# Both heads' sums from the exponentials, x rounded on VectorE, and attention visits by twos in an attention and gated feed-forward kernel

## The chip, the cores and the metric

The kernel runs on one core of a Trainium2 chip. The core has a matrix engine (TensorE, PE in the profile), three engines for elementwise work (VectorE or DVE, ScalarE or ACT, GpSimd or POOL), and SyncE (SP), which here issues the DMA transfers in order. Each engine runs its own instructions in order and waits for other engines by semaphores. Operands lie in SBUF, results of matmuls in PSUM, and large arrays in DRAM. The metric is the device time of one execution in microseconds.

## The reference

Causal attention over a sliding window of 64 positions feeds a gated feed-forward layer:

```python
# q, k, v: 8 batches, 8 heads, 576 positions, 64 values; float32
scores = matmul(q, k.T) / sqrt(64)
scores = where((rel >= 0) & (rel < 64), scores, -1e9)      # rel: position of q minus position of k
attn = exp(scores - max(scores))
attn = attn / (sum(attn) + 1e-9)
x = matmul(attn, v)                                        # laid out as 4608 tokens x 512
gate = 1 / (1 + exp(-(x @ w_gate)))                        # 512 x 1536
out = (gate * (x @ w_val)) @ w_out                         # 1536 x 512
```

The three weight arrays come as 64-bit floats; all else is float32, and so is the result.

## The kernel before

**Tiles and numbers.** The 4608 tokens stand in 12 tiles of 384, taken in 6 pairs of tiles s = 0 to 5. The 8 heads stand in 4 pairs p. A tile with a pair of heads is a unit of attention, written (t, p): eight units for a pair of tiles. Matmuls that need float32 accuracy split both operands into a rounded part and a remainder and make three products of them; a rounded part is a conversion to the type fp32r, a remainder is one subtraction behind it.

**A unit of attention** goes over the engines so. TensorE makes the scores of both heads (L224) in blocks of 128x128. VectorE scales and masks a block and takes its minimum (L249, with a read of the minimum). ScalarE takes the exponential (L257) and, where `accum_out` is given, the row's sum with it, which a second short instruction reads out (ACTIVATION_READ_ACCUMULATOR). VectorE inverts the sums (L264, L265), GpSimd or VectorE multiplies (L274), TensorE transposes (L328), ScalarE copies the transposes to SBUF (L333), TensorE multiplies them with v (L358). In the first two tiles the second head's exponentials leave no sum; VectorE adds it up with a reduction instead (L270). There the outputs of L358 become a tile of x directly: ScalarE rounds them out of PSUM (L365), VectorE subtracts (L366).

**The order of the whole.** The first pair's attention comes first, on its own. Then come its up products (L394), gate and product (L402, L407), the split of the hidden values (L420, L422) and its down products (L442); the weights are meanwhile converted from their 64-bit halves, in a step a on ScalarE (L117, L118), a step b on VectorE (L126, L128, L130) and a step c (ScalarE's rounding L158, VectorE's remainder L159, and stores). From the second pair on, up and down products are made by a scheme of seven products for eight (`product`, L619; k = 0 to 5 numbers blocks of the hidden size, n = 0 to 6 the products), with sums of weights that GpSimd makes in the second pair (L541 to L547, split by L554 and L561) out of rows loaded again from DRAM (L531), and weights loaded for each k and n (L468). The attention of the next pair of tiles is fed in between these products. Such a place is called a visit here; a dictionary `fill` holds them under the key ("u", 7k + n), and `attend` puts them into the order.

Two forms of visit exist. `stage_s` takes one unit: the outputs of the unit before it, then its own scores, copies and exponentials, its normalization and transposes later. `stage_v` takes two units at once, and copies a whole 128x384 tile of outputs (L311) where `stage_s` copies three pieces (L289, L290, L295). The second pair of tiles uses `stage_s`, later pairs `stage_v`.

What sets the order: every step is put into a table of events with a time, a rank and a function; the table is sorted, and the language's scheduler then places instructions by its own simulated times. Matmuls keep the order of the program. `tc.issue_after(ins)` places instructions behind `ins` on the engine of `ins` only; the conversions of weights use it with `marks`, where each tile of x leaves the instructions that made it.

## Time and profile before

| | |
|---|---|
| median of three runs | 949.63 us (948.51 to 950.33) |
| the profiled execution | 950.16 us, of which 948.2 are the span from first to last instruction |
| granted TensorE clock, mean | 0.997 |
| busy: PE, PEld, DVE | 934.0, 898.5, 712.2 us |
| busy: ACT, POOL | 502.7, 150.7 us |
| DMA | 273.45 MB, mean 288 GB/s |

A row of a timeline gives the start, the length, the engine, the line of the kernel, the operation, result and operands, the shape and the number of instructions taken together; in square brackets stand the idle time before it and what ended it. Rows of groups give busy time and mean nanoseconds of one instruction. The length of an instruction overlaps the next one's start by some hundredths to a tenth of a microsecond, so that a pitch is read from start to start. SPq stands for SP's issues of transfers, and a DMA's landing is counted from its issue.

### The profile page before, as it was taken

To read this page: it belongs to the slowest core of one execution; us is meant where nothing else is said; L and a number is where in the kernel's file an instruction comes from. 1 tells how busy PE (TensorE), PEld (TensorE's weight loads), DVE (VectorE), ACT (ScalarE), POOL (GpSimd) and SP (SyncE) were. 2 spreads that over 40 slices of the span, in tenths; PEclk is the share of its full clock that TensorE was granted. 3 is DMA by queue.
4 is the path that set the end of the run, shared out by engine and by line. 5 is a ranking of instruction groups with operands and counts; after the bars stand their busy time and mean duration, and the time that the engine had idled before them with its cause. 6 is when DMAs were issued, how large, how long until landed. Compare 5 with 4: busy or idle time off the path is not lost.

```text
span 948.2 us, 20297 instructions
## 1 busy us (share of the span) xinstructions
PE 934.0 (99%) x7164; PEld 898.5 (95%) x7164; DVE 712.2 (75%) x1919; ACT 502.7 (53%) x1374; POOL 150.7 (16%) x232
## 2 busy tenths in 40 slices
PE   6999999999999999999999999999999999999998
PEld 5899999889999999999999999999999999999998
DVE  6989989787888975666875677786566796566882
ACT  7866776655666653545553455454455565222460
POOL 4201104604773000311000113000111100000000
PEclk9999999999999999999999999999999999999999
DMA  9899998989999988888879788788888678988474
GB/s 327 311 383 358 368 321 282 359 292 358 386 315 315 407 288 288 287 271 270 264 252 317 251 291 290 258 251 296 287 267 269 221 247 273 299 260 250 130 214 164
DMA packets 105509, 273.45 MB, mean 288 GB/s; under 512 B 11456, under 2 KB 33600, under 8 KB 105408
## 3 DMA queue, kind: packets, MB, share of 16 engines
q1 hardware_dynamic: 105408, 272.15, 85.4%
q8 instruction: 57, 0.93, 0.4%
q14 instruction: 44, 0.36, 0.1%
HBM read 220.20 MB, written 51.90 MB: 287 GB/s over the span
## 4 chain that ended last, share of the span: by engine, by line
PE 92%; DMA 4%; DVE 3%; ACT 1%; issue 0%; SPq 0%; DVEq 0%; ACTq 0%
PE pr L619 45%; PE y L619 23%; PE ph L394 10%; PE y L442 4%; PE pp L328 3%; PE pr L358 2%; PE s L224 1%; DMA raw<-in_moe_w_gate_dram 1%; PE pr L224 1%; DMA a<-w32d 1%; DMA wt<-wd 1%; PE oo L358 1%; DMA wd<-ws 1%; PE s L358 1%; DVE p L249 1%; DMA out_dram<-yo 0%
## 5 line engine op out<-in xcount | busy, mean ns | idle before, releaser
L619 PE MATMUL pr<-x_T,wt 128*128 128x384 f32 x1224 | 224.4, 335 | 0.0
L619 PE MATMUL y<-h,wot 128*128 128x384 f32 x1260 | 220.4, 335 | 0.0
L619 PEld LDWEIGHTS y<-h,wot 128*128 128x128 f32 x1260 | 218.3, 188 | 1.3 <-DVE h L407 1.2
L619 PEld LDWEIGHTS pr<-x_T,wt 128*128 128x128 f32 x1224 | 212.6, 188 | 0.3 <-issue 0.3
L619 PE MATMUL pr<-x_B,wt 128*128 128x384 f32 x1008 | 188.7, 338 | 0.6 <-DMA wt<-wd 0.6
L619 PEld LDWEIGHTS pr<-x_B,wt 128*128 128x128 f32 x1008 | 174.4, 188 | 3.3 <-issue 2.1
L701 ACT CAST h<-h 128x384 fp32r<-128x384 f32 x210 | 104.8, 514 | 97.7 <-PE y L619 42.7
L274 POOL TENSOR_TENSOR p<-p,rs 128x384 f32<-128x384 f32 x76 | 69.4, 926 | 524.6 <-DVE rs L265 388.5
L702 DVE TENSOR_TENSOR h<-h,h 128x384 fp32r<-128x384 f32 x210 | 110.2, 552 | 23.4 <-ACT h L701 23.1
L257 ACT ACTIVATE p<-p,mn 128x128 f32<-128x128 f32 x288 | 110.8, 392 | 19.8 <-DVE mn L249 19.1
L394 PE MATMUL ph<-x,w 128*128 128x384 f32 x576 | 106.1, 338 | 0.1
L402 ACT ACTIVATE g<-c 128x384 f32<-128x384 f32 x90 | 46.9, 522 | 108.0 <-DVE c L658 96.2
L394 PEld LDWEIGHTS ph<-x,w 128*128 128x128 f32 x576 | 99.8, 188 | 2.6 <-issue 1.0
L629 DVE TENSOR_TENSOR c<-pr,p 128x384 f32<-128x384 f32 x60 | 33.0, 551 | 46.4 <-PE pr L619 46.4
L407 DVE SCALAR_TENSOR_TENSOR h<-g,c 128x384 f32<-128x384 f32 x90 | 50.1, 557 | 5.9 <-DVE c L658 0.5
L333 ACT COPY p<-pp 128x384 f32<-128x384 f32 x80 | 34.4, 479 | 30.6 <-PE pp L328 29.8
L257 ACT ACTIVATION_READ_ACCUMULATOR p<-p,mn 128x1 f32 x264 | 49.8, 189 | 0.0
L634 ACT COPY p<-pr 128x384 f32<-128x384 f32 x60 | 27.2, 472 | 37.8 <-PE pr L619 37.8
L629 DVE TENSOR_TENSOR u<-pr,p 128x384 f32<-128x384 f32 x60 | 33.1, 552 | 16.0 <-PE pr L619 15.8
L328 PE MATMUL pp<-ident,p 128*128 128x128 f32 x288 | 41.6, 281 | 1.8 <-POOL p L274 1.3
L658 DVE TENSOR_TENSOR c<-pr,p 128x384 f32<-128x384 f32 x60 | 33.1, 555 | 10.2 <-PE pr L619 9.8
L619 PE MATMUL pr<-x_T,ws 128*128 128x384 f32 x216 | 40.3, 338 | 0.0
(186 smaller groups left out, 1216.9 us busy)
## 6 DMA issues: line engine op xcount, KB each, us to landing
wt<-wd SPq DMA_DIRECT2D x186, 512.0 KB, 4.5
wot<-wod SPq DMA_DIRECT2D x105, 512.0 KB, 4.6
v<-in_vN_dram SPq DMA_DIRECT2D x48, 384.0 KB, 5.6
wd<-ws SPq DMA_DIRECT2D x48, 256.0 KB, 5.1
k<-in_kT_dram SPq DMA_DIRECT2D x48, 224.0 KB, 5.9
q<-in_qT_dram SPq DMA_DIRECT2D x48, 192.0 KB, 5.7
w32d<-w SPq DMA_DIRECT2D x36, 256.0 KB, 5.0
wd<-w SPq DMA_DIRECT2D x36, 256.0 KB, 5.6
```

What stands on the lines that cost most here:

```text
L257: exp = nc.scalar.activation(pt[:, u, :], pt[:, u, :], AF.Exp, bias=mn[:, u:u + 1], scale=-1.0, **sums)
L274: eng.tensor_mul(out=pt, in0=pt, in1=rs.unsqueeze(2).broadcast_to([P, UP, P]))
L328: pe(nc.tensor.transpose(pp[:, u, :], pt[:, u, :], ident))
L358: pe(nc.tensor.matmul(oo[U // 2][h * BLK:(h + 1) * BLK, U % 2 * BLK:(U % 2 + 1) * BLK], vt[:, U, h * BLK:(h + 1) * BLK], pT[h][:, U // 2, ...
L394: pe(nc.tensor.matmul(ph, l, r, start=i == 0, stop=i == len(prs) - 1))
L402: act = nc.scalar.activation(g, c, AF.Tanh)
L407: nc.vector.scalar_tensor_tensor(out=out, in0=g, scalar=1.0, in1=val, op0=ALU.add, op1=ALU.mult)
L442: pe(nc.tensor.matmul(yb[y], l, r, start=first and n == 0, stop=last and n == 2))
L619: pe(nc.tensor.matmul(ps, l, r, start=first and i == 0, stop=last and i == 2, skip_group_check=not check))
L629: marks["plus"] = nc.vector.tensor_add(out=o, in0=ps, in1=a).ins
L701: nc.scalar.copy(h2[:, 0, :], src)
L702: nc.vector.tensor_sub(out=h2[:, 1, :], in0=src, in1=h2[:, 0, :].bitcast(F32))
```

## The change

Four edits stand in it.

1. In the first two tiles both heads' exponentials give their sums; the eight reductions L270 are gone, and 24 more sums are read out on ScalarE.
2. x is rounded by VectorE, which also subtracts: the conversion out of PSUM leaves ScalarE.
3. What a tile of x leaves in `marks` is now the last copy of transposes on ScalarE and both of VectorE's instructions. A weight conversion that was to stand behind a tile of x thereby stands behind the copy on ScalarE, and behind the split on VectorE.
4. In the second pair of tiles the visits at 4 and 9 stay single; from 19 on they are `stage_v`: units 3 and 4 are taken at 19 (with the outputs of unit 2), units 5 and 6 at 26, unit 7 at 33, and the last outputs at 40. Before, single visits stood at 14, 19, 25, 30 and 35, and the last outputs at 41. `stage_v` now also takes one unit or none.

```diff
-                sums = {} if t < 2 and h else {"accum_out": rs[:, u:u + 1]}
                 exp = nc.scalar.activation(pt[:, u, :], pt[:, u, :], AF.Exp, bias=mn[:, u:u + 1],
-                                           scale=-1.0, **sums)
+                                           scale=-1.0, accum_out=rs[:, u:u + 1])
...
     def normalize(t, p, h):
         pt, rs = st[(t, p, h)], sums_of[(t, p)][:, h, :]
-        if t < 2 and h:
-            nc.vector.reduce_sum(out=rs, in_=pt, axis=mybir.AxisListType.X)
         if t < 4:
             invert(rs)
...
-            c, d = new
+            c, d = new[0], new[-1]
...
-            scores(*d, (True, False, True) * 2)
+            if len(new) > 1:
+                scores(*d, (True, False, True) * 2)
             scores(*c)
...
-            for u in (d, c):
+            for u in new[::-1]:
...
     def x_split(src, nm, i, eng):
         x2 = xp.tile([P, 2, TT], F32R, name=f"x_{nm}", tag=f"x{i}")
-        hi = nc.scalar.copy(x2[:, 0, :], src)
+        hi = eng.tensor_copy(out=x2[:, 0, :], in_=src)
         lo = eng.tensor_sub(out=x2[:, 1, :], in0=src, in1=x2[:, 0, :].bitcast(F32))
-        marks[nm] = (hi.ins, lo.ins)
+        marks[nm] = (marks["pTv"], hi.ins, lo.ins)
...
-    VISITS = (4, 9, 14, 19, 25, 30, 35)
...
-            for v, u in enumerate(VISITS, 1):
+            for v, u in enumerate((4, 9), 1):
                 visit(("u", u), 3, *unit(s + 1, v), unit(s + 1, v - 1), u % NPR)
                 visit(("u", u + 1), 4, *unit(s + 1, v))
                 visit(("u", u + 3.5), 1, *unit(s + 1, v))
-            visit(("u", 41), 2, *unit(s + 1, 7))
+            for u, new, done in ((19, (3, 4), (2,)), (26, (5, 6), (3, 4)), (33, (7,), (5, 6)), (40, (), (7,))):
+                new, done = ([unit(s + 1, i) for i in x] for x in (new, done))
+                visit(("u", u), 5, new, done)
+                for a, tn, tb in zip(new[::-1], (1.5, 2.5), (3.5, 5)):
+                    visit(("u", u + tn), 4, *a)
+                    visit(("u", u + tb), 1, *a)
```

Three places where instructions move. First ScalarE, at the last unit of the first pair, (1, 3), whose exponentials are `p_1_3`; `oo` are outputs of L358, `w` and `raw` belong to the weight conversion. Before:

```order
L257 ACTIVATE p_1_3_751<-p_1_3_751,mn_1_3_752 128x128 x2
L365 CAST x_0_724<-oo_0_711 128x384
L257 ACTIVATE p_1_3_751<-p_1_3_751,mn_1_3_752 128x128
L333 COPY pT_1_1_731<-pp_1_1_727 128x384
L333 COPY pT_1_1_737<-pp_1_1_733 128x384
L365 CAST x_1_795<-oo_1_782 128x384
L117 ACTIVATE w_0_1_838<-raw_1_336 128x512
L118 ACTIVATE raw_1_336<-raw_1_336 128x512
L333 COPY pT_1_2_802<-pp_1_2_798 128x384
L333 COPY pT_1_2_808<-pp_1_2_804 128x384
L333 COPY pT_1_3_814<-pp_1_3_810 128x384
L333 COPY pT_1_3_820<-pp_1_3_816 128x384
```

The same place with the change:

```order
L256 ACTIVATE p_1_3_744,rs_3_734<-p_1_3_744,mn_1_3_745 128x128 x3
L331 COPY pT_1_1_724<-pp_1_1_720 128x384
L331 COPY pT_1_1_730<-pp_1_1_726 128x384
L117 ACTIVATE w_0_1_830<-raw_1_334 128x512
L118 ACTIVATE raw_1_334<-raw_1_334 128x512
L331 COPY pT_1_2_794<-pp_1_2_790 128x384
L331 COPY pT_1_2_800<-pp_1_2_796 128x384
L331 COPY pT_1_3_806<-pp_1_3_802 128x384
L331 COPY pT_1_3_812<-pp_1_3_808 128x384
```

The casts of x have left the queue, and the weight conversion L117, L118 follows the copies of unit 1 directly.

Second VectorE behind the last exponentials of that unit; x_0 to x_3 are tile 1's four parts of x. Before:

```order
L366 TENSOR_TENSOR x_0_724<-oo_0_711,x_0_724 128x384
L270 TENSOR_REDUCE rs_3_741<-p_1_3_751 128x3
L264 SCALAR_TENSOR_TENSOR rs_3_741<-rs_3_741 128x3
L407 SCALAR_TENSOR_TENSOR h_0_0_776<-g_0_671,ph_0_0_763 128x384
L265 RECIPROCAL rs_3_741<-rs_3_741 128x3
L420 CAST hh_0_778<-h_0_0_776 128x384
L422 TENSOR_TENSOR hl_0_779<-h_0_0_776,hh_0_778 128x384
L366 TENSOR_TENSOR x_1_795<-oo_1_782,x_1_795 128x384
L126 TENSOR_SCALAR zz_1_841<-w_0_1_838 128x512
L128 SCALAR_TENSOR_TENSOR w_0_1_838<-w_0_1_838,zz_1_841 128x512
L130 ISA w_0_1_838<-raw_1_336,w_0_1_838 128x1024
L159 TENSOR_TENSOR w_1_845<-w_0_1_838,w_1_845 128x2x256
```

With the change, from the last inversion on:

```order
L405 SCALAR_TENSOR_TENSOR h_0_0_768<-g_0_665,ph_0_0_755 128x384
L418 CAST hh_0_770<-h_0_0_768 128x384
L363 CAST x_1_787<-oo_1_774 128x384
L420 TENSOR_TENSOR hl_0_771<-h_0_0_768,hh_0_770 128x384
L364 TENSOR_TENSOR x_1_787<-oo_1_774,x_1_787 128x384
L126 TENSOR_SCALAR zz_1_833<-w_0_1_830 128x512
L128 SCALAR_TENSOR_TENSOR w_0_1_830<-w_0_1_830,zz_1_833 128x512
L363 CAST x_2_827<-oo_2_814 128x384
L130 ISA w_0_1_830<-raw_1_334,w_0_1_830 128x1024
L364 TENSOR_TENSOR x_2_827<-oo_2_814,x_2_827 128x384
L363 CAST x_3_855<-oo_3_842 128x384
L364 TENSOR_TENSOR x_3_855<-oo_3_842,x_3_855 128x384
```

The conversions of x (L363) now stand between, and the remainder of the weight (L159) comes behind x_3, where it stood ahead of x_2.

Third SP's queue at k = 3 of the second pair. `wt_1_3_4` are the weights of product n = 4, `a0` and `a1` rows of weights for GpSimd's sums, `wd` stores, q, k and v inputs of units. Before:

```order
L531 DMA a1_1_4_3843<-w32d_1_10_135 128x512
L481 DMA wd_3_6_176<-ws2_1_3_3917 128x512
L180 DMA q_5_1_4183<-in_qT_dram 128x384
L468 DMA wt_1_3_4_3930<-wd_3_4_174 128x1024
L531 DMA a0_0_5_4010<-w32d_0_5_118 128x512
L468 DMA wt_1_3_5_3943<-wd_3_5_175 128x1024
L181 DMA k_5_1_4184<-in_kT_dram 128x448
```

With the change:

```order
L479 DMA wd_3_6_176<-ws2_1_3_3871 128x512
L180 DMA q_4_3_3996<-in_qT_dram 128x384
L529 DMA a1_1_4_3869<-w32d_1_10_135 128x512
L181 DMA k_4_3_3997<-in_kT_dram 128x448
L180 DMA q_5_1_4000<-in_qT_dram 128x384
L181 DMA k_5_1_4001<-in_kT_dram 128x448
L466 DMA wt_1_3_4_3884<-wd_3_4_174 128x1024
L529 DMA a0_0_5_4004<-w32d_0_5_118 128x512
L466 DMA wt_1_3_5_3901<-wd_3_5_175 128x1024
```

Loads for two units, q and k each, stand ahead of the weights of n = 4, with the row block L529 among them; before, one q did.

## The prediction

> **What bounds the kernel now.** I read the busy times on the page first, then the start by windows, then the timelines of the two places that the change touches, engine by engine.
>
> ```profile
> span 948.2 us, 20297 instructions
> PE 934.0 (99%) x7164; PEld 898.5 (95%) x7164; DVE 712.2 (75%) x1919; ACT 502.7 (53%) x1374; POOL 150.7 (16%) x232
> ```
>
> TensorE is busy for 99% of the span. Where it has idle time and who is late there, the windows of the start show (columns: stretch, its length, busy time of PE, PEld, DVE, ACT, POOL, then granted clock, DMA share, GB/s):
>
> ```profile
> 10.00:20.00 10.00, 8.92 (x128) 6.80 (x121) 8.22 (x48) 9.63 (x34) 4.94 (x6) 1.00 1.04 399
> 20.00:30.00 10.00, 8.84 (x119) 7.51 (x119) 9.93 (x54) 9.75 (x37) 3.98 (x6) 0.83 1.01 374
> 30.00:40.00 10.00, 9.11 (x133) 7.55 (x133) 8.78 (x31) 7.71 (x24) 4.09 (x5) 1.00 0.88 333
> 40.00:50.00 10.00, 10.00 (x77) 9.62 (x74) 9.10 (x18) 8.30 (x16) 0.00 (x0) 1.00 0.85 267
> ```
>
> From 10 to 30 us VectorE and ScalarE are both full; at 30 to 40 both have gaps, and TensorE is 0.89 us short. From 40 on TensorE has no idle time: there a gain needs fewer or denser matmuls, while before that it needs TensorE's inputs sooner. The stretch from 30 to 40 is the last unit of the start, tile 1 with head pair 3. How TensorE comes out of it, in an order that the change leaves alone:
>
> ```profile
> 38.79 2.05 PE L358 MATMUL oo<-pT,v 128*64 128x64 f32 x48 [0.61 <-ACT pT L333]
> 40.77 8.81 PE L394 MATMUL ph<-x,w 128*128 128x384 f32 x48
> ```
>
> The outputs of units 2 and 3 (48 matmuls) end at 40.77, and the first up products that need tile 1 begin. A faster start has to move this row.
>
> **The start: what the three edits cost.** Prices, by groups:
>
> ```profile
> L270 DVE TENSOR_REDUCE rs<-p 128x3 f32<-128x384 f32 x8 | 4.3, 540 | 1.4 <-ACT p L257 1.4
> L365 ACT CAST x<-oo 128x384 fp32r<-128x384 f32 x8 | 3.6, 466 | 1.0 <-PE oo L358 1.0
> L366 DVE TENSOR_TENSOR x<-oo,x 128x384 fp32r<-128x384 f32 x8 | 4.3, 544 | 0.6 <-ACT x L365 0.6
> L420 DVE CAST h<-h 128x384 fp32r<-128x384 f32 x10 | 3.8, 380 | 0.1
> L257 ACT ACTIVATION_READ_ACCUMULATOR p<-p,mn 128x1 f32 x264 | 49.8, 189 | 0.0
> ```
>
> VectorE loses eight reductions (L270) and gains eight conversions out of PSUM, which before does not show. The nearest rows are L420, the same conversion out of SBUF (0.380 us), and L366, the subtraction that reads the same PSUM tile (0.544 us). I take L366's price since its source is the one the new instruction reads; then eight for eight is a wash (0.54 against 0.54). At L420's price VectorE gains 8 x 0.16 = 1.3 us, of which only what falls in the last unit reaches the end. A rule of the Trainium skill bears on it, *VectorE: DVE Perf Modes*, section "Why PSUM operands drop a tier": an operand in PSUM keeps fp32 work at the basic rate. By it the price is L366's and the sum the one below; without it the price is L420's and the sum that of rival 1. The pair of rows fits the rule, but the trace of before has no such conversion.
>
> ScalarE loses eight casts and gains 24 accumulator reads. With and without a read the exponentials stand like this:
>
> ```profile
> 32.50 0.40 ACT L257 ACTIVATE p<-p,mn 128x128 f32<-128x128 f32 x1 [1.17 <-DVE mn L249]
> 33.67 0.68 ACT L257 ACTIVATE p<-p,mn 128x128 f32<-128x128 f32 x2
> 34.26 0.46 ACT L365 CAST x<-oo 128x384 fp32r<-128x384 f32 x1
> 34.62 0.40 ACT L257 ACTIVATE p<-p,mn 128x128 f32<-128x128 f32 x1
> 36.75 0.48 ACT L365 CAST x<-oo 128x384 fp32r<-128x384 f32 x1 [1.00 <-PE oo L358]
> 37.13 0.69 ACT L117 ACTIVATE w<-raw 128x512 f32<-128x512 f32 x1
> 38.28 1.60 ACT L333 COPY pT<-pp 128x384 f32<-128x384 f32 x4
> ```
>
> Three with a read take 1.17 (32.50 to 33.67, the two behind the first being left out here), 0.39 each; two without take 0.59 (33.67 to 34.26), 0.30 each. A read adds 0.09, 24 add 2.2, and the casts give back 8 x 0.36 (34.26 to 34.62) = 2.9. Before 32 us lie 21 of the reads (1.9) and some six of the casts (2.2): next to nothing on ScalarE, nothing on VectorE, so I leave the last unit's first exponential where it is, at 32.50.
>
> Behind it ScalarE does six exponentials with reads, 32.50 + 6 x 0.39 = 34.84 (before 34.92: 34.62 + 0.30, with a cast between), and two copies of unit 2's transposes (0.40 each, from the four at 38.28) until 35.6. Before, it then stood 1.00 us for the outputs of unit 2 because the cast of x came ahead of the first weight conversion. Now that cast is VectorE's, and the conversion (L117 and L118, 37.13 to 38.28, 1.15) fills the hole: done at 36.75 where it was 38.28. What the four copies behind it wait for then is the last head's normalized exponentials:
>
> ```profile
> 31.56 0.46 DVE L264 SCALAR_TENSOR_TENSOR rs<-rs 128x3 f32<-128x3 f32 x1
> 35.22 0.54 DVE L270 TENSOR_REDUCE rs<-p 128x3 f32<-128x384 f32 x1
> 36.85 1.07 DVE L422 TENSOR_TENSOR hl<-h,hh 128x384 fp32r<-128x384 f32 x1
> 41.56 1.01 DVE L366 TENSOR_TENSOR x<-oo,x 128x384 fp32r<-128x384 f32 x2
> 42.95 0.69 DVE L128 SCALAR_TENSOR_TENSOR w<-w,zz 128x512 int32<-128x512 int32 x1
> 43.55 0.42 DVE L126 TENSOR_SCALAR zz<-w 128x512 int32<-128x512 int32 x1
> 43.89 0.68 DVE L130 CUSTOM_DVE_ANT_0 w<-raw,w 128x1024 uint16<-128x1024 uint16 x1
> 36.68 0.83 POOL L274 TENSOR_TENSOR p<-p,rs 128x384 f32<-128x384 f32 x1 [1.51 <-DVE rs L265]
> ```
>
> That multiplication ends at 37.51. With the sums ready at 34.9, VectorE inverts them by about 35.7 and POOL ends at 36.6; transposes, copies from 36.95 to 38.5, outputs, and TensorE could start the up products at about 39.4, 1.4 earlier than 40.77.
>
> But those products need all four tiles of x, and VectorE is now the maker of both halves. Its queue from 35.7 on, at the pitches of the rows above (0.45 for a conversion or subtraction, from the two that take 1.01 together; L128 0.60 and L126 0.34 from start to start; L130 0.60, its length being L128's): the gate product, which reads PSUM too, 36.2; h's conversion, held beside POOL until 36.6, to 37.1; x_1 37.55; h's remainder 38.0; x_1's remainder 38.45; L126 38.8; L128 39.4; x_2 39.85; L130 40.45; x_2's remainder 40.9; x_3 41.35; its remainder 41.8. The eleventh of the first twelve up products needs this last one, so the twelve end at 41.8 + 2 x 0.17 = 42.15. Before, the last remainder landed at 41.56 + 1.01 = 42.57, and the twelve ended at about 42.9. **Gain 0.8 us.** Bounds: 1.4 if VectorE keeps up; 0 if the queue up to 32 us gets longer by what is saved here, or if the weights, converted in the order of arrival behind it, come no earlier. A loss is rival 3.
>
> **The visits by twos.** One single visit in the second pair of tiles, and one double visit as they stand in the third:
>
> ```profile
> 219.37 2.24 PE L619 MATMUL pr<-x_B,wt 128*128 128x384 f32 x12
> 225.41 2.24 PE L619 MATMUL pr<-x_B,ws 128*128 128x384 f32 x12
> 227.49 2.24 PE L619 MATMUL pr<-x_B,wt 128*128 128x384 f32 x12
> 390.31 2.25 PE L619 MATMUL pr<-x_T,wt 128*128 128x384 f32 x12
> 392.49 1.62 PE L358 MATMUL pr<-p,v 128*64 128x64 f32 x48
> 394.04 0.67 PE L224 MATMUL pr<-k,q 64*64 64x128 f32 x16
> 395.51 4.45 PE L619 MATMUL pr<-x_B,wt 128*128 128x384 f32 x24
> 399.80 3.29 PE L619 MATMUL pr<-x_T,wt 128*128 128x384 f32 x18
> ```
>
> Twelve dense products take 227.49 - 225.41 = 2.08. From 219.37 to 225.41 lie 24 of them and one single visit: 6.04 - 4.16 = 1.88. From 390.31 to 399.80 lie 36 and a double one: 9.49 - 6.24 = 3.25, which is 1.55 of outputs, 1.47 of scores and 0.23 of entering and leaving. Replaced are five single visits, 5 x 1.88 = 9.40, by three: one unit's outputs with two units' scores, half of 1.55 plus some 0.08 of its own start, 0.85 + 1.47 + 0.23 = 2.55; 3.25; and two units' outputs with one unit's scores, 1.55 + 0.80 + 0.23 = 2.58. Together 8.38; the last unit's outputs stay alone. **Gain 1.0 us.** The matmuls stay, so only entering and leaving is saved. Bounds: 1.5 if the first and the third visit enter and leave for nothing (0.23 each); 0 if products behind a double visit wait for its copies, which in the row at 395.51 they don't (24 in 4.29, twice 2.08 and 0.13).
>
> The visits' work on VectorE and ScalarE is the same in number; TensorE covers it with the products between visits. SP's queue, though, is reordered: the load of the weights for k=3, n=4 (L468) now stands behind the loads of unit 4's k and of unit 5's q and k, and behind a load (L531) that waits for POOL to give a buffer back. As it was, POOL's splitting of one set of sums, SP's issue, the product, and the landing times of L468 in this stretch:
>
> ```profile
> 255.93 2.15 POOL L561 TENSOR_TENSOR ws<-sw,ws 128x128 fp32r<-128x128 f32 x4
> 266.09 0.38 SPq L468 DMA_DIRECT2D wt<-wd  x1
> 274.13 2.24 PE L619 MATMUL pr<-x_B,wt 128*128 128x384 f32 x12
> DMA to landing us min/median/max: 5.3/6.6/10.6
> ```
>
> Issued at 266.09 and taking 6.6, it landed at about 272.7, 1.4 ahead of its product. In the change that product comes earlier by 0.8 from the start and by 1.88 for the single visit at 25 that falls away, less 2.55 - 1.88 = 0.67 for the bigger one at 19: at 274.13 - 2.0 = 272.1. If the buffers come free no later than TensorE's own earlier progress gives them, the issue is earlier by about 0.7 as well, lands at 272.0, and the product waits for nothing. I price it at nothing; the cover is 0.1 us wide, and its cost without is the slower rival.
>
> **Sum.** The profiled execution took 950.16 (span 948.2, and 2.0 around it), 0.53 above the median of the three, 949.63. -0.8 - 1.0 = -1.8: 948.4 against its own time, and **947.8** against the median.
>
> **Rivals.** (1) *The whole start gain comes through*, 1.4, because the conversion out of PSUM costs nearer to L420's 0.380, and up to 32 us VectorE gains some of the 1.3 as well: 949.63 - 1.0 - 1.4 to 2.5 = 946.1 to 947.2, take 946.8. For it: VectorE at 9.93 is the fuller engine. Against: ScalarE is as full, 9.75.
> (2) *Nothing comes of the start*, since VectorE has the same work and the conversions end when they did: 948.6. For it: the equal prices; against: the 1.00 us hole on ScalarE at 36.75 does go.
> (3) *VectorE is shut out while POOL multiplies.* The inversion at 31.56 takes 0.46 for 128x3 elements and the subtraction at 36.85 takes 1.07 against 0.54 of the group of L366, ending 0.41 behind POOL's multiplication (37.51). A reduction is not held so (35.22, 0.54). Without reductions in between, the second head's inversion falls into the first head's multiplication in each of seven units; at 0.3 to 0.5 each, a third of it on the path, that is 7 x 0.4 / 3 = 0.9, which eats the start's 0.8: 948.7; with all of it on the path, 7 x 0.4 = 2.8, and 950.6. The Trainium skill has this, *SBUF — State Buffer*, section "Who interferes with whom": VectorE with two SBUF inputs and GpSimd exclude one another for a whole instruction, and a reduction never takes part; the rows agree.
> (4) *Slower: TensorE waits for the weights of k=3, 4 and 5 behind the loads of the double visits.* The place is the queue above: SP issues in order, so a load that waits for its buffer holds the weights. POOL now splits one set of sums (the 2.15 at 255.93) before it makes the sums whose buffer the load L531 waits for. If the whole chain of these loads comes 2.15 later by that, and two issues more stand ahead of the weights (2 x 0.38), the cover of 0.1 leaves 2.8 us of waiting at k=3; at each of the next two k one q and one k more stand ahead, 0.76 less the 0.1: 0.7. Together 4.2: 949.63 - 1.8 + 4.2 = 952.0. It decides once the waits sum to more than 1.8, for k=3 alone from an issue after 272.1 - 6.6 + 1.8 = 267.3. For it: three loads more stand ahead. Against: before, the median landing left 1.4 us to spare.
>
> **How the numbers follow.** About 0.2% (1.9 us) is what a measurement of this kernel can tell from no change: faster is below 947.7, slower above 951.5. Forecast (-1.2 to -2.4) 0.42, of which 0.22 lie below 947.7; rival 1 0.22, all faster; rival 2 0.18, no change; rival 3 0.06, no change; rival 4 0.12, slower. So faster 0.44, same 0.44, slower 0.12. The range 946.0 to 950.3 leaves out rival 4 and the far ends of rivals 1 and 3; the forecast's own is 947.2 to 948.5.
>
> **What would show it.** The first twelve up products of tile 1 end 0.8 earlier than 42.9 (1.4: rival 1; not earlier: rival 2). The conversion L117 stands at 35.6 with no wait for the outputs ahead. The new conversion's mean is near 0.54. The three double visits add 2.55, 3.25 and 2.58 to the dense products around them. A wait of TensorE for weights at k=3, n=4 is rival 4; inversions of 0.4 us and more are rival 3. I am wrong if the start moves by over 1.5 either way, if the visits save under 0.5, or if TensorE has a new wait of over 0.5.

## The result and the profile after

| | before | changed |
|---|---|---|
| median | 949.63 us (948.51 to 950.33) | 954.81 us (953.60 to 957.17) |
| ratio | 1 | 1.0057 [1.0046, 1.0068] |
| the profiled execution | 950.16, span 948.2 | 953.82, span 952.0 |
| granted TensorE clock, mean | 0.997 | 1.000 |

The change is slower by 5.2 us; 947.8 was forecast, and the time lies outside the predicted range. The profiled execution is the lowest but one of its five, 1.0 below their median, and that of the kernel before lay 0.5 above its own. So the spans differ by 3.8 us only, and some 1.4 of the medians' 5.2 stand in neither trace. The page of the changed kernel:

```profile
span 952.0 us, 20303 instructions
PE 931.3 (98%) x7164; PEld 895.8 (94%) x7164; DVE 712.8 (75%) x1919; ACT 501.6 (53%) x1380; POOL 150.5 (16%) x232
```

TensorE has the same 7164 matmuls and less busy time than before (931.3 against 934.0); what is longer is its waiting. The windows of the changed kernel say where (columns as in the prediction):

```profile
50.00:60.00 10.00, 9.18 (x67) 7.69 (x65) 6.11 (x18) 5.98 (x14) 0.00 (x0) 1.00 0.90 328
70.00:80.00 10.00, 9.24 (x88) 8.23 (x87) 9.49 (x22) 6.32 (x13) 0.00 (x0) 1.00 1.03 383
80.00:90.00 10.00, 8.04 (x48) 7.55 (x47) 9.16 (x28) 8.67 (x26) 2.39 (x2) 1.00 1.02 379
```

Two of the same stretches before:

```profile
50.00:60.00 10.00, 10.00 (x75) 9.27 (x74) 8.03 (x26) 7.03 (x18) 0.00 (x0) 1.00 1.00 372
80.00:90.00 10.00, 10.00 (x71) 9.05 (x71) 9.73 (x21) 6.10 (x17) 1.93 (x2) 1.00 0.99 361
```

From 40 to 90 us TensorE had no idle time before. Now it has 0.82 between 50 and 60, 0.76 between 70 and 80 and 1.96 between 80 and 90, and in the first of these VectorE too did less than before, 6.11 against 8.03. The order of TensorE's products is the same but for the visits, so that the start of each can be set against the start of the same one before (minus is earlier):

| start before, us | 40.8 | 44 | 60 | 67 | 76 | 84 | 89 | 229 | 329 | end |
|---|---|---|---|---|---|---|---|---|---|---|
| shift, us | -1.39 | -0.85 | +1.06 | +1.09 | +2.05 | +4.25 | +4.04 | +3.97 | +3.82 | +3.80 |

The start came 0.85 earlier. Then 1.9 us went between 44 and 60, and 2.95 between 67 and 89; the visits (229 to 329) brought back 0.15. The rows of TensorE in the changed kernel that carry this:

```profile
39.39 2.34 PE L392 MATMUL ph<-x,w 128*128 128x384 f32 x10
41.88 6.85 PE L392 MATMUL ph<-x,w 128*128 128x384 f32 x38
...
53.86 2.73 PE L392 MATMUL ph<-x,w 128*128 128x384 f32 x14
56.74 2.60 PE L392 MATMUL ph<-x,w 128*128 128x384 f32 x12 [0.16 <-DVE w L159]
60.12 2.02 PE L392 MATMUL ph<-x,w 128*128 128x384 f32 x10 [0.78 <-DVE w L159]
...
74.62 0.45 PE L356 MATMUL ph<-p,v 128*64 128x64 f32 x8 [0.76 <-ACT g L400]
...
77.99 6.43 PE L392 MATMUL ph<-x,w 128*128 128x384 f32 x36
86.39 2.36 PE L392 MATMUL ph<-x,w 128*128 128x384 f32 x12 [1.96 <-ACT g L400]
```

and in the kernel before, where none of these waits stands:

```profile
54.52 6.54 PE L394 MATMUL ph<-x,w 128*128 128x384 f32 x36
...
75.95 8.55 PE L394 MATMUL ph<-x,w 128*128 128x384 f32 x48
```

Below, the loss between 44 and 60 is called the first part (up products of the third block wait for weights), that between 67 and 89 the second part (at 74.62 outputs of a visit, at 86.39 up products wait for a gate that has still to read the PSUM bank they write).

**The first part.** VectorE of the changed kernel, from 50 us on:

```profile
54.59 0.43 DVE L126 TENSOR_SCALAR zz<-w 128x512 int32<-128x512 int32 x1 [3.32 <-ACT w L117]
54.93 0.68 DVE L128 SCALAR_TENSOR_TENSOR w<-w,zz 128x512 int32<-128x512 int32 x1
...
56.00 0.68 DVE L159 TENSOR_TENSOR w<-w,w 128x512 fp32r<-128x512 f32 x1
...
59.38 0.68 DVE L159 TENSOR_TENSOR w<-w,w 128x512 fp32r<-128x512 f32 x1
```

The program's names say whose these are. The step at 54.59 belongs to `w_2_1`, weights of a down product; the one at 54.93 to `w_1_2`, 56.00 is the remainder of `w_0_2` and 59.38 that of `w_1_2`, both of which the up products need next. In the order before, `w_1_2`'s L128 (51.83) and `w_0_2`'s remainder (53.46) stand ahead of `w_2_1`, whose L126 comes at 54.34; the last row is `w_1_2`'s remainder:

```profile
51.83 0.69 DVE L128 SCALAR_TENSOR_TENSOR w<-w,zz 128x512 int32<-128x512 int32 x1
53.46 0.69 DVE L159 TENSOR_TENSOR w<-w,w 128x512 fp32r<-128x512 f32 x1 [0.95 <-ACT w L158]
...
56.35 0.68 DVE L159 TENSOR_TENSOR w<-w,w 128x512 fp32r<-128x512 f32 x1
```

`w_2_1` was late because ScalarE, in its own order, stood for a load ahead of it (the row at 53.14, raw weights of `w_1_3`):

```profile
53.14 0.68 ACT L118 ACTIVATE raw<-raw 128x512 int32<-128x512 uint32 x1 [2.60 <-DMA raw<-in_moe_w_val_dram]
53.89 0.66 ACT L117 ACTIVATE w<-raw 128x512 f32<-128x512 f32 x1
54.46 0.61 ACT L158 CAST w<-w 128x512 fp32r<-128x512 f32 x1
```

So VectorE stood 3.32 us at a step that nobody needed yet, with the steps behind it that TensorE did need. `w_1_2` was ready at 59.38 + 0.68 = 60.06 instead of 57.03, three later.

A second swap bears on the same weights, on ScalarE. The first step of `w_0_3`, which waits for a store, now stands ahead of the rounding of `w_1_2` (58.06):

```profile
57.11 0.67 ACT L117 ACTIVATE w<-raw 128x512 f32<-128x512 f32 x1 [1.35 <-DMA w32d<-w]
```

Before, the rounding came first (55.40, L117 at 56.30). In the change VectorE ended its step b of `w_1_2` only at 57.9, so that the two swaps hold the rounding about equally long; e9 and e14 below tell them apart.

**The second part.** ScalarE of the changed kernel around the gate of tile 1's block 3, and the same gate before:

```profile
80.07 0.40 ACT L256 ACTIVATE p<-p,mn 128x128 f32<-128x128 f32 x1 [2.17 <-DVE mn L249]
...
84.80 0.60 ACT L158 CAST w<-w 128x512 fp32r<-128x512 f32 x1
85.31 0.65 ACT L117 ACTIVATE w<-raw 128x512 f32<-128x512 f32 x1
85.87 0.46 ACT L400 ACTIVATE g<-ph 128x384 f32<-128x384 f32 x1
```

```profile
76.63 0.40 ACT L257 ACTIVATE p<-p,mn 128x128 f32<-128x128 f32 x1 [0.63 <-DVE mn L249]
...
81.61 0.48 ACT L402 ACTIVATE g<-ph 128x384 f32<-128x384 f32 x1
```

The gate starts 4.26 later: 3.44 because the exponentials ahead of it start later (they wait for VectorE's minima; VectorE did 1.9 us less between 50 and 60 than before, and from 66 us to those minima it worked with only 0.5 of idle time), and 0.82 because two steps of conversions, the rounding of `w_2_3` (84.80) and L117 of `w_1_5` (85.31), now stand ahead of the gate on ScalarE. TensorE itself was 2.04 late at that point (77.99 against 75.95). 4.26 - 2.04 = 2.22, less some 0.25 that it had to spare before, is the wait of 1.96. The 0.76 at 74.62 is the same thing one gate earlier: the gate of tile 0's block 3 starts 2.05 later than before (74.10 against 72.05), where TensorE was 1.09 late. ScalarE had stood 1.16 for VectorE at the rounding of `w_2_2` (70.38), which now goes ahead of a copy of transposes and of four steps of conversions on the way to that gate.

### The profile page after: what moved, and what is told of

It is laid out like the page before. It is cut to its first block, busy times and chain, and to the rows that moved or that the text cites. A ratio compares the mean times of both kernels' runs of the same rounds, so it can differ in the third digit from the quotient of the medians.

```text
span 952.0 us, 20303 instructions
## 1 busy us (share of the span) xinstructions
PE 931.3 (98%) x7164; PEld 895.8 (94%) x7164; DVE 712.8 (75%) x1919; ACT 501.6 (53%) x1380; POOL 150.5 (16%) x232
## 4 chain that ended last, share of the span: by engine, by line
PE 83%; DMA 6%; DVE 5%; ACT 2%; issue 1%; POOL 1%; SPq 1%; DVEq 0%; POOLq 0%; ACTq 0%
PE pr L617 41%; PE y L617 23%; PE ph L392 7%; PE y L440 4%; PE pp L326 2%; PE pr L356 2%; ACT p L256 2%; DMA a<-w32d 1%; DMA raw<-in_moe_w_val_dram 1%; PE s L224 1%; PE pr L224 1%; DMA wt<-wd 1%; DMA wa<-w32d 1%; DMA wd<-ws 1%; DVE p L249 1%
## 5 line engine op out<-in xcount | busy, mean ns | idle before, releaser
L256 ACT ACTIVATION_READ_ACCUMULATOR p<-p,mn 128x1 f32 x288 | 54.5, 189 | 0.0
```

The source lines that it names most:

```text
L256: exp = nc.scalar.activation(pt[:, u, :], pt[:, u, :], AF.Exp, bias=mn[:, u:u + 1], scale=-1.0, accum_out=rs[:, u:u + 1])
```

## The experiments

Eighteen kernels ran, each beside the kernel before on the same chip. Times are medians; "shift" is the start of TensorE's products against the same ones before, from the two traces, as in the table above. All compute the whole reference.

**The edits apart.** First the sums alone (edit 1).

> Only edit 1: both heads' sums come from the exponentials, the eight reductions are gone; x is still rounded on ScalarE, the visits stay single. Theory (the loss of the whole change comes from the order of the weight conversions behind tile 1, which this edit leaves word for word as before): no stall of TensorE between 50 and 90 us, 0 to 0.8 us faster than before, ratio 0.999 to 1.000. Rival (the 24 more accumulator reads hold up ScalarE and with it the start and the gates): 1 us slower or more.

949.77 against 949.89, ratio 1.0001 [0.9992, 1.0010]; the shift at 44 us is -0.05. No gain by itself, and no new wait from 40 us on.

Next edits 2 and 3 alone, x rounded on VectorE with the new `marks`.

> Only edits 2 and 3: x is rounded on VectorE and the conversions are ordered behind copies; the reductions and the single visits stay. From tile 1 on VectorE's and ScalarE's orders are those of the whole change. Theory: nearly the whole loss is here, 4 to 5 us slower than before (the stalls at 56 to 60, 74 and 84 us come again), ratio 1.004 to 1.005. Rival (sums): within 1 us of before.

955.34 against 949.89, 1.0061 [1.0048, 1.0073]. The shift is +0.63 at 44 (VectorE has the conversions more and no reduction less), +1.06 at 64 to 70, +5.46 at 89, and the row of the gate is that of the whole change:

```profile
86.23 3.91 PE L394 MATMUL ph<-x,w 128*128 128x384 f32 x12 [1.95 <-ACT g L402]
```

The wait is that of the change. That the twelve products behind it take 3.91, where the change has 2.36, is the clock: the granted clock of this trace is 0.83 between 80 and 90 us, 1.00 in the change, so that some 1.55 of the 5.46 belong to this one execution. The first part is 0.43 only, because the start came 1.5 later here; TensorE is at +1.06 at 60 us in both. The loss comes with these two edits. The 0.85 of the start needs both: the conversions put on VectorE and the reductions taken away.

Edit 2 with `marks` as before, that is without edit 3:

```diff
-        marks[nm] = (marks["pTv"], hi.ins, lo.ins)
+        marks[nm] = (hi.ins, lo.ins)
```

> Only edit 2: x is rounded on VectorE, with the marks as before, so that weight conversions on ScalarE are no longer tied to tile 1's rounding. ScalarE's order has w_2_1's first step ahead of w_0_2's rounding, VectorE's has w_0_2's remainder behind the first step of w_2_1 only. Theory (loss by order): part of the loss, 1 to 3 us slower than before. Rival (the loss needs the marks of edit 3): within 1 us of before.

960.18 against 949.07, 1.0113 [1.0098, 1.0128], worse than expected and in another place. A conversion now goes ahead of the copies of transposes on ScalarE and waits there for its load; the waits of TensorE show it:

```profile
PE oo L358 <- ACT pT L333: 9.1, 3, 8.2
```

So edit 3 is what edit 2 needs, and is not itself the fault.

The visits alone (edit 4).

> Only edit 4: visits by twos in the second pair; the start is as before. Theory: the visits save 0.9 us of TensorE's time and lose 0.3 to 0.6 of it to a wait for weights, so 0.3 to 0.6 faster. By the prediction's sum 1.0 faster; by its fourth rival 2 to 3 slower, with a wait for weights at k=3, n=4.

950.01 against 949.89, 1.0001 [0.9992, 1.0010]. The gain is there and is eaten by two waits, of which the first is new by 0.4 only (the kernel before has 0.62 at the same product, at 239.15):

```profile
239.25 2.32 PE L620 MATMUL pr<-x_B,wt 128*128 128x384 f32 x12 [1.03 <-ACT xf L295]
294.10 2.38 PE L620 MATMUL pr<-x_B,wt 128*128 128x384 f32 x12 [1.45 <-DMA wt<-wd]
```

The second is at k = 4, n = 4. Its weights were issued at 286.58, behind the loads of q and k for units (5, 3) and (6, 0), whose buffer comes free only with the scores of the visit at 26.

**The first part: who stands behind whom.** The change, with all steps of `w_2_1` placed behind `w_0_2`'s step c, on ScalarE behind its rounding and on VectorE behind its remainder:

```diff
-        marks[("w", i)] = (cp,)
+        marks[("w", i)] = cp[:1] if i != 6 else cp
...
-        return cp.ins
+        return cp.ins, sub.ins
...
+                if a[0] == 5:
+                    early += (("w", 6),)
```

The weight tiles are numbered here in the order of their conversion: 3 is `w_0_1`, 5 `w_2_1`, 6 `w_0_2`, 7 `w_1_2`, 9 `w_0_3`, 11 `w_2_3`, 13 `w_1_4`, 16 `w_1_5`; what stands in `early` is what a step is placed behind.

> The whole change, but the conversion of the third weight's block 1 (w_2_1) is ordered behind the rounding and the remainder of block 2 of the first weight (w_0_2) on ScalarE and on VectorE, as it stood before the change. Nothing else is written differently. Theory (the stalls begin where that conversion, waiting for a store, stands ahead of w_0_2): w_0_2 is ready some 2 us sooner, the stall before 60 us goes, and with it most of the loss: 949 to 951. Rival (the weights arrive too late whatever the order, since the transfer of raw weights landed at 53.1 instead of 52.2): still 953 or more.

950.10 against 949.89, 1.0000 [0.9991, 1.0009]. No loss from 44 to 81 us, 0.21 at the gate; `w_1_2` was ready at 56.18. The loss of 5 us hangs on that order. But the start's 0.85 shrank to 0.11: in the order that came out, a remainder of `w_0_1` went ahead of x_3, and TensorE waits 0.77 for x at 42.61.

The kernel before, with one swap on ScalarE (`w_0_2`'s rounding behind `w_2_1`'s L117, which `marks` now holds; not shown is a line that gives step c another time and rank in the table of events). On VectorE `w_2_1`'s L126 thereby comes ahead of `w_0_2`'s remainder, but stays behind `w_1_2`'s L128:

```diff
+                if a[0] == 6 and f is conv_c:
+                    early += (("a", 5),)
```

> The kernel before, with one thing changed: the rounding of w_0_2 on ScalarE is put behind the first step of w_2_1, as in the whole change. x, sums and visits are as before. Theory (that swap alone starts the stalls): w_0_2 and w_1_2 are ready 1 to 2 us later and the kernel is 1 to 2 us slower. Rival (the swap only hurts together with a start that comes out earlier or a busier VectorE): no difference, 949.6 to 950.2.

950.22 against 949.07, 1.0009 [1.0000, 1.0018]; no wait between 50 and 60. This swap makes no wait of TensorE there, and no difference of more than the interval's 1.7 us.

e4 with `w_0_1`'s remainder put back behind x_3 (again without the line that gives it another time in the table):

```diff
+                if a[0] == 3 and f is conv_c:
+                    early = ("1_3",)
```

> The kernel of e4_order, and the remainder of the weight w_0_1 on VectorE stands behind the last tile of x, as in the whole change, instead of ahead of it. Theory: the start keeps the 0.85 us that the whole change had at 44 us (e4_order had 0.11 there), with the conversions still in the order of before; if the rest of the start has room for it, the time is 0.7 below e4_order, about 949.4; if the conversions of the weights set the pace up to 90 us whatever the start, the gain is eaten by 90 us and the time is that of e4_order.

950.30 against 949.07, 1.0013 [1.0005, 1.0022]. The start's -0.83 is still -0.64 at 55. But VectorE stands at `w_0_2`'s remainder for ScalarE's rounding, `w_1_2` is ready at 59.18, and the shift at 67 is +1.63:

```profile
53.51 0.69 DVE L159 TENSOR_TENSOR w<-w,w 128x512 fp32r<-128x512 f32 x1 [2.87 <-ACT w L158]
```

The step at which VectorE stands is another one; what it stands for is still ScalarE behind a load, and the rounding of `w_1_2` (57.19) still stands behind L117 of `w_0_3`, which waits 1.03 for its store.

The change with one constraint on VectorE, L126 of `w_2_1` behind L128 of `w_1_2` (left in `marks` as "b"):

```diff
+                if a[0] == 5 and f is conv_b:
+                    early += (("b", 7),)
```

> The whole change with one constraint on VectorE alone: the first step of w_2_1 (L126) stands behind the sign step of w_1_2 (L128), where in the whole change it stood ahead of it; ScalarE keeps the change's order up to the exponentials of the first visit. Theory (VectorE standing for 3.3 us at the step of w_2_1, with w_1_2 and w_0_2 queued behind, starts the loss): no VectorE wait of 3 us at 51 to 55 us with w_1_2 behind it, w_1_2 ready by 58 instead of 60.1, the stalls at 60, 74 and 84 us go, and the time is 949 to 950.5. Rival (ScalarE's order, with w_2_1 ahead of w_0_2's rounding, is enough): 952 or more.

950.59 against 949.57, 1.0011 [1.0002, 1.0020]. The gates' waits are gone, the one for weights is not (0.76 at 59.72, shift +1.79 at 67): the time came as expected, the mechanism by half. What is left is the second swap by itself: VectorE was done with step b of `w_1_2` at 55.6, and ScalarE stood at `w_0_3` for the store before it rounded `w_1_2`:

```profile
56.74 0.66 ACT L117 ACTIVATE w<-raw 128x512 f32<-128x512 f32 x1 [1.36 <-DMA w32d<-w]
...
57.68 0.61 ACT L159 CAST w<-w 128x512 fp32r<-128x512 f32 x1
```

e6 with, besides, `w_0_3`'s steps behind those of `w_1_2`, on ScalarE behind its rounding and on VectorE behind its remainder:

```diff
-        marks[("w", i)] = cp[:1] if i != 6 else cp
+        marks[("w", i)] = cp[:1] if i not in (6, 7) else cp
...
+                if a[0] == 9:
+                    early += (("w", 7),)
```

> The kernel of e6_xfirst (the start's 0.85 us kept), and the first step of w_0_3 stands behind the rounding and remainder of w_1_2 on ScalarE and VectorE as before the change. Theory (in e6_xfirst and e9_dveorder w_1_2 came at 59.2 and 59.7 us, since its remainder stood behind w_0_3's step, which waits for a store): w_1_2 by 57.5, no stall at 60 us, and the 2.5 us lost at 55 to 67 shrink to 1 or less: 948.5 to 949.3. Rival (the weights come no sooner, whatever the order, and the start's gain can't be kept): 950.2 as e6_xfirst.

951.33 against 949.47, 1.0019 [1.0010, 1.0028]. This one has no first part (shift -0.45 at 44, -0.27 at 55 and at 70; `w_1_2` ready at 57.48), and yet the second:

```profile
84.04 2.37 PE L392 MATMUL ph<-x,w 128*128 128x384 f32 x12 [1.45 <-ACT g L400]
```

**The second part: lateness and order.** The change, with weight steps kept behind the gates of block 3 on ScalarE. Of these constraints those for `w_1_4` and `w_1_5` took hold; the rounding of `w_2_3` still stands ahead of the gate of tile 1.

```diff
+        marks[("g", t, j)] = (act.ins,)
...
+                if f is not conv_b:
+                    if a[0] in (11, 16):
+                        early += (("g", 1, 3),)
+                    if a[0] == 13:
+                        early += (("g", 0, 3),)
```

> The whole change; only on ScalarE two gates of tile 0 and tile 1 (block 3) are kept ahead of the steps of later weight conversions (w_1_4; w_2_3's rounding and w_0_5, w_1_5's steps), everything up to 70 us stays in the order of the change. Theory (the loss has two parts: 1.9 us at 55 to 67 us by late weights, and 2.9 us at 73 to 90 us by gates that stand behind conversions on ScalarE): the first part stays, the second goes: 2.2 to 2.9 below the whole change, 952.0 to 952.6. Rival (the second part is VectorE's backlog after the first, whatever ScalarE's order): no change, 954 or more.

950.17 against 949.47, 1.0011 [1.0002, 1.0020]. The shift at 89 is -0.03 where the change had +4.04. Both parts are nearly gone, though only the second was worked on (the profiled execution is the fastest of its eleven). Up to 69 us VectorE and ScalarE have the same order as in the change, but the load that ScalarE stands for landed at 51.8 instead of 53.1, so that VectorE's wait at `w_2_1` was 2.23:

```profile
53.23 0.43 DVE L126 TENSOR_SCALAR zz<-w 128x512 int32<-128x512 int32 x1 [2.23 <-ACT w L117]
```

`w_1_2` was ready at 58.71 and the first part cost 0.46. Its size hangs on when that load lands. It was issued at 45.2 in the trace of before, 46.5 here and 47.2 in the change.

All the traces side by side tell order and load apart. Counted from the moment ScalarE gets to the step that needs this load (53.14 in the change), `w_1_2` was ready

| kernels | us later |
|---|---|
| before, e1, e3, e4, e5, e11, e12, e16 | 4.76 to 4.88 |
| e14, e15, e18 | 5.92 to 5.93 |
| change, e2, e13, e17 (one order on both engines from 42 to 69 us) | 6.86 to 6.95 |

e6 and e10 with orders of their own also come to 6.9; e7, e8 and e9 lie between 5.6 and 7.6. So of the three us by which `w_1_2` was late in the change, 2.1 are the order (6.92 against 4.79), and 0.9 are ScalarE getting there at 53.14 instead of 52.24.

The kernel before, with tile 1's gate put behind L117 of `w_1_5` and the rounding of `w_2_3`:

```diff
+        late = {(0, 3): (("a", 13),), (1, 3): (("a", 16), ("w", 11))}.get((t, j), ())
+            for ins in [i for nm in late for i in marks.get(nm, ())]:
+                behind.enter_context(tc.issue_after(ins))
```

> The kernel before, with one thing changed: on ScalarE the gate of tile 1, block 3, stands behind the first step of w_1_5 and the rounding of w_2_3, as in the whole change. Theory (a gate behind conversions on ScalarE costs TensorE what those conversions take and wait): in before the two took 81.98 to 83.05 behind the gate, so the gate comes some 1.1 to 1.5 us later, TensorE stalls for it at 82 to 84 us and the time is 0.7 to 1.5 longer, 950.2 to 951.0. Rival (it needs VectorE's backlog): no stall, no difference.

950.53 against 949.44, 1.0008 [0.9999, 1.0016], no wait at the gate:

```profile
80.27 0.70 ACT L117 ACTIVATE w<-raw 128x512 f32<-128x512 f32 x1
80.84 0.64 ACT L158 CAST w<-w 128x512 fp32r<-128x512 f32 x1
81.35 0.52 ACT L406 ACTIVATE g<-ph 128x384 f32<-128x384 f32 x1
```

Its exponentials also came 1.2 earlier against TensorE than before, so it shows that the place alone need not cost anything, not that it never does. Eight traces together say more. With T the start of TensorE's products of block 3 (the row at 77.99), E that of the unit's first exponential (80.07) and G that of the gate (85.87):

| kernel | E - T | G - E | G - T | wait shown |
|---|---|---|---|---|
| before | 0.68 | 4.98 | 5.66 | none |
| change | 2.08 | 5.80 | 7.88 | 1.96 |
| e4 | 0.88 | 5.24 | 6.12 | 0.21 |
| e9 | 0.17 | 5.24 | 5.41 | none |
| e13 | 1.39 | 4.68 | 6.07 | 0.18 |
| e14 | 1.57 | 5.79 | 7.36 | 1.45 |
| e16 | -0.55 | 6.06 | 5.51 | none |
| e18 | 0.24 | 4.68 | 4.92 | none |

In all four that wait, G - T less the wait is 5.9; in the four that don't, G - T is below 5.9. The wait is what is over, and the other twelve traces fall the same way. The 5.9 is a sum: 36 products take 6.27 where nothing waits, a product's length is 0.17 longer than the step to the next, and the product that waits starts 0.52 after the gate does. So the gate is all that this product waits for. E - T is how far the attention's exponentials lag behind TensorE (in the change because of VectorE's minima), G - E the order on ScalarE (4.7 to 5.0 with four steps of conversions ahead of the gate, 5.2 with five, 5.8 to 6.1 with six), and the change made both longer, by 1.40 and 0.82, where 0.25 was to spare. That is the whole of the 1.96.

**The loads of the visits.** e4 with loads of q and k for (4, 3), (5, 1), (5, 3) and (6, 0) placed behind the weight loads on SP:

```diff
-        nc.sync.dma_start(out=qt, in_=qT[rows, c0:c0 + TT])
-        nc.sync.dma_start(out=kt, in_=kT[rows, c0:c0 + TT + BLK])
+        with tc.issue_after(marks["w_load"]) if (t, p) in ((4, 3), (5, 1), (5, 3), (6, 0)) else nullcontext():
+            nc.sync.dma_start(out=qt, in_=qT[rows, c0:c0 + TT])
+            nc.sync.dma_start(out=kt, in_=kT[rows, c0:c0 + TT + BLK])
```

> The kernel of e4_order, and the loads of q and k for the units of the last two visits and for the first of the next pair stand behind the weight loads of their k on SP's queue instead of ahead. Theory (the wait for weights at k=4, n=4, 0.44 us in e4_order and 1.45 in e3_visits, is SP standing at loads of q whose buffer the visit ahead holds): the wait goes, the visits then gain about 0.9 to 1.0, and the time is 0.4 to 0.6 below e4_order: about 949.6. Rival (the buffers of the weights themselves come late): the wait stays and nothing moves.

956.00 against 949.07, 1.0071 [1.0058, 1.0083]. Up to 329 us the shift goes from +0.20 to -1.62, the gain as hoped and no wait for weights; then the load of k for (6, 0), which I had moved too far, comes behind the weights of the next pair and costs it all:

```profile
PE pr L225 <- DMA k<-in_kT_dram: 5.3, 1, 5.3
```

The runs below take the same edit without (6, 0). On e9:

> The kernel of e9_dveorder, and the loads of q and k for the units of the last two visits of the second pair stand behind that k's weight loads on SP's queue (not the first load of the pair behind, which e5_loads had moved too far). Theory: the visits gain 1.4 to 1.8 instead of 0.5, as the trace of e5_loads has it up to 329 us: 948 to 949, and 0.8 to 1.2 below e9_dveorder. Rival: the late load of q or k stalls a visit and nothing is gained.

951.07 against 949.57, 1.0013 [1.0004, 1.0022]; the visits take the shift from +3.29 to +1.87, which the time does not show.

On the visits alone:

> Only edit 4 with the same order of loads; the start is that of before. Theory: 1.4 to 1.8 faster than before, 948.0 (e3_visits without the loads: no difference). By the prediction's sum for the visits, 1.0 faster.

949.49 against 949.57, 0.9994 [0.9985, 1.0003]; +0.38 to -0.21, no wait for weights at k = 4, one of 0.66 at k = 1.

On sums and visits, without edits 2 and 3:

> Edits 1 and 4 with the same order of loads; x is rounded on ScalarE as before. Theory (the conversion of x on VectorE is what reorders the weight conversions; the sums alone change nothing there): the time of e11_visits_loads or up to 0.4 below, 947.6 to 948.2.

949.02 against 949.57, 0.9991 [0.9982, 1.0000]; shift -2.33 at 329.

On e14, on e13, and on e14 with the constraints of e13:

> The kernel of e14_allorder with the order of loads of e10_both, e11 and e12. Theory: 0.6 to 1.4 below e14_allorder, 947.5 to 948.5, and faster than before by more than its interval. Rival (the visits' gain is taken back by the waits at k=1 and k=4): the time of e14_allorder.

950.68 against 949.47, 1.0017 [1.0009, 1.0026]: the gate's wait is again 1.50, the visits go from +1.13 to -0.37.

> The kernel of e13_gates with the order of loads of e10, e11, e12 and e15. Theory: the visits' gain comes in, 0.6 to 1.2 below e13_gates: 949.0 to 949.6.

948.77 against 949.44, 0.9998 [0.9988, 1.0008]. The profiled execution is the slowest of its twelve (951.73). VectorE and ScalarE have e13's order from first to last, and the load of `w_1_3` was issued at 46.5 as in e13; but it landed at 52.7 instead of 51.8, `w_1_2` was ready at 59.72 instead of 58.71, and the first part cost 1.49 instead of 0.46. At the gate only 0.17 was waited, and the visits take the shift from +2.63 to +1.71.

> All constraints found so far on the whole change: conversions in the order of e14_allorder, gates ahead as in e13_gates, loads as in e17. Theory (both parts of the loss gone, the start's 0.8 and the visits' 1.0 kept): 947.4 to 948.4, below every kernel so far and faster than before by more than its interval. Rival (the start's gain is lost again between 44 and 90 us, since the weights' pace does not depend on it): 948.8 to 949.5, as e12_sums_visits.

948.69 against 949.44, 0.9991 [0.9983, 1.0000]. No wait of TensorE for the weights of up products or for gates is left, only one of 0.47 stands at k = 1; the shift is -0.69 at 44, -0.73 at 89, -0.83 at 229 and -1.90 at 329. This is the change as the prediction had thought of it, 6.1 us below the change as it is, and at the edge of what can be told from no change. The time lies between the two that were expected; in the trace the start's gain is not lost between 44 and 90 us, so the rival's reason is not the one.

## Why the prediction was wrong

**The failed step** is in the costing of the start: "0 if the queue up to 32 us gets longer by what is saved here, or if the weights, converted in the order of arrival behind it, come no earlier. A loss is rival 3." The weights came later, not "no earlier", and no rival held it. Edit 3 and the new places of the conversions were costed by what they do to the last unit of the start, and the queues of VectorE and ScalarE behind it were taken as they were. The changed order, which could be read before the run, had `w_2_1` ahead of `w_1_2` on VectorE, and on ScalarE `w_0_3` ahead of the rounding of `w_1_2` and `w_1_5` ahead of the gate, and the trace of before had the row on which such a move turns, ScalarE standing for the same load:

```profile
52.24 0.68 ACT L118 ACTIVATE raw<-raw 128x512 int32<-128x512 uint32 x1 [1.25 <-DMA raw<-in_moe_w_val_dram]
```

The term put at 0 measured 1.9 + 2.95 = 4.85 us. With the start's -0.85 and the visits' -0.15 that is the 3.8 by which the two traces differ; part of it, as e13 and e17 show, changes with the landing from one execution to the next.

Shown by the runs: that the loss comes with edits 2 and 3 (e2), that it goes when `w_2_1`'s steps stand behind (e4), that at the gate lag and order add up (the table of eight), and that without waits of either kind a gain of the forecast's size comes back in the trace (e18, -1.9), though not in the medians (-0.75).

**The start** was right. Point by point: the twelve first up products were to end 0.8 earlier, and the shift at 44 is 0.85. The new conversion was priced at 0.54 from the subtraction's row:

```profile
L363 DVE CAST x<-oo 128x384 fp32r<-128x384 f32 x8 | 4.4, 547 | 0.0
```

0.547, where the same conversion out of SBUF took 0.380 before. This is the case that the Trainium skill states (*VectorE: DVE Perf Modes*, "Why PSUM operands drop a tier"), and rival 1 falls with it. L117 was to stand at 35.6 with no wait for outputs ahead, the last remainder of x was to end at 41.8:

```profile
35.23 0.68 ACT L117 ACTIVATE w<-raw 128x512 f32<-128x512 f32 x1
```

```profile
41.27 0.56 DVE L364 TENSOR_TENSOR x<-oo,x 128x384 fp32r<-128x384 f32 x1
```

It ended at 41.83. Rival 2 (nothing from the start) falls, for the edits together; for the sums alone it would have been right (e1), and edits 2 and 3 alone lose 0.63 there (e2).

The clock could have made this gain, since the kernel before had a granted clock of 0.83 between 20 and 30 us and the change 1.00. It did not: e13 had 0.83 there and e17, with the same order, 1.00, and at 44 us they are 0.74 and 0.75 ahead. One reading in the prediction was wrong without consequence: from 10 to 20 us VectorE was not full, but busy for 8.22 of 10.

**Rival 3** has a true mechanism and no weight. The inversion of the last unit took 0.73 instead of 0.15, beside a multiplication on POOL, both ending within 0.02 of each other:

```profile
34.63 0.73 DVE L263 SCALAR_TENSOR_TENSOR rs<-rs 128x3 f32<-128x3 f32 x1 [0.29 <-ACT p L256]
```

```profile
34.51 0.83 POOL L271 TENSOR_TENSOR p<-p,rs 128x384 f32<-128x384 f32 x1 [2.08 <-DVE rs L264]
```

That fits the exclusion in *SBUF — State Buffer*, "Who interferes with whom", of the Trainium skill. It did not eat the start's gain. Of the sixteen inversions of the start it is the only one of over 0.4, where the rival had one in each of seven units and the kernel before had three.

**The visits** were sized nearly right. The three double ones, in the changed kernel:

```profile
260.79 2.25 PE L617 MATMUL pr<-x_T,wt 128*128 128x384 f32 x12
...
267.58 2.24 PE L617 MATMUL pr<-x_B,wt 128*128 128x384 f32 x12
...
279.30 2.25 PE L617 MATMUL pr<-x_T,wt 128*128 128x384 f32 x12
...
286.83 2.24 PE L617 MATMUL pr<-x_B,wt 128*128 128x384 f32 x12
...
298.98 2.25 PE L617 MATMUL pr<-x_T,wt 128*128 128x384 f32 x12
...
305.73 2.24 PE L617 MATMUL pr<-x_B,wt 128*128 128x384 f32 x12
```

Between the starts of the two rows of each lie 24 products, twice 2.08, and the visit: 6.79 - 4.16 = 2.63, 7.53 - 4.16 = 3.37 and 6.75 - 4.16 = 2.59, together 8.59 against 8.38 forecast and 9.40 before. So 0.8 was saved, of 1.0. Mis-sized was the term put at nothing, SP's queue. The mechanism of rival 4 came, at k = 4 instead of 3 and for 0.16 to 1.45 instead of 2.8 (0.16 in the change, whose visits come later against the loads than in e3). A wait at k = 1 grew beside it, to 0.89 in the change; it is not of the visits' making, since the kernel before has 0.62 there and e1 0.69. In the change the products fall back 0.27 more at k = 1 and 0.40 at k = 4, which left 0.15 of the 0.8. Taken out by the order of loads, the same visits moved the shift by 0.9 to 1.5 (e10, e12, e15, e17, e18), and by 0.6 alone (e11).

The test named for being wrong, a new wait of TensorE of over 0.5, was met by three rows.

**What stays open.** The traces of e12 and e18 end 2.4 and 1.9 us before that of the kernel before, the medians only 0.55 and 0.75. Of this, 0.5 is that the trace of before comes from an execution above its median and 0.5 to 1.4 that theirs come from ones below; why the spread is that wide is not known. The granted clock does not sort it: executions of the kernel before with 1.000 took from 947.71 to 951.57. What moves the landing of the load that ScalarE waits for is open too: issued at 46.5 in e13 and in e17, it landed 0.9 apart. No run moved that landing by itself; that the first part follows it is read from four traces of one order.

## What to carry to other kernels

When an edit moves where one kind of instruction may stand, read the whole order of each in-order engine behind the place, until it agrees with the old one again. A step that waits for a transfer, put ahead of one that the bound engine needs soon, costs its whole wait less the cover, and the lost time of the engine that stands there comes back later as lag in every queue that it feeds. To size such a wait, add lag and order and take off the slack: here one threshold, 5.9 us from product to gate, told waiting from not waiting in all twenty traces. Loads whose buffer is given back late belong behind the loads of weights on the same queue, but one load moved too far cost more (5.3 us) than all the others brought.

## What had not been expected of the hardware

Three kernels with one order on VectorE and ScalarE up to 69 us (the change, e17 and e13) lost 1.9, 1.49 and 0.46 us in the first part, and what differs in their traces there is one load, which landed at 53.1, 52.7 and 51.8. Nothing else went against what had been expected of the engines: the price of the one new kind of instruction came out within 0.01 us.
